# One table set for logarithms and exponentials, loaded by name, in an attention and SwiGLU kernel

## The chip, the cores and the metric

The kernel runs on one core of a Trainium2 chip. The metric is device time in microseconds of that core for one execution; the time before is the median of three runs. The engines are named as in the profile: PE (TensorE: matrix products), DVE (VectorE), ACT (ScalarE: activation functions, copies and some DMA issues), POOL (GpSimd) and SP (SyncE: issues most DMAs).

## The reference

Queries and keys are normalised row by row, attention runs over 8 batches with 12 heads, 448 positions and 64 columns, and its result goes through a SwiGLU block:

```python
def rmsnorm(x, g):
    rms = np.sqrt(np.mean(x * x, axis=-1, keepdims=True) + 1e-06)
    return x / rms * g
q_n, k_n = (rmsnorm(q, g_q), rmsnorm(k, g_k))
scores = scale * np.matmul(q_n, k_n.transpose(0, 1, 3, 2))
attn = np.exp(scores - np.max(scores, axis=-1, keepdims=True))
attn = attn / (np.sum(attn, axis=-1, keepdims=True) + 1e-09)
x = np.matmul(attn, v)          # then (B,H,S,D) -> (B*S, H*D) = (3584, 768)
g = x @ w_gate                  # w_gate, w_val: (768, 1536); w_out: (1536, 768)
silu = g * (1.0 / (1.0 + np.exp(-g)))
return silu * (x @ w_val) @ w_out
```

## The kernel before, in words

Two heads of one batch are a pair; there are 48 pairs. `attention(m)` adds the work of pair `m`: load queries and keys, square them on ACT, sum the squares on DVE, exchange partial sums between the partitions by four small copies on ACT (`ss`, L766), take one over the root (`inverse_root`), scale on POOL (L783), transpose on DVE, scale the queries on ACT (L802). Then come the scores on PE (L828, into the PSUM tile `st`, of which there are two), the exponentials on ACT (`exps`, L843, into `es`, `gt` or `more`), the weighted values on PE (L904, into `at`), the sums of the weights on PE (L928), their reciprocals on DVE (`rd`, L963), a copy (L983), an addition and a division.

`inverse_root` computes the root as exp(-0.5 ln(x)): a logarithm (L666) and an exponential (L667) of 28 columns on ACT, and an improvement on DVE (L672 to L674). ACT evaluates a function from the table set that is in use; where an activation needs a function of another set, the program has an `ACT_TABLE_LOAD` ahead of it, which the profile shows with the line of that activation. Silu (L1351) has a set of its own.

`block(n)` adds the SwiGLU block of two batches: up products (L1277) from weights in `ws` and inputs in `xs`, read out of PSUM by copies on ACT (L1238) and additions on DVE (L1240, L1242, L1244), then silu, then down products (L1456). Both matrix products are done by a scheme with 15 products for 9 blocks, whose combined weights are made by `convert` from raw 64-bit weights (loads L1104, ACT L1112 and L1116, DVE, POOL), stored to DRAM and loaded again as pieces of `ws` (L1372 for up, L1442 for down; two buffers).

The order on each engine is set by a planner, `Order`. Every step is added with its engine, an assumed duration, a due time (`when`), a `rank` that moves it ahead, what it follows, and the buffers that it takes and uses. `run` picks the steps one after the other; the program then has each engine's instructions in that order. A step may carry a `mode`; where it differs from its engine's mode, `SWITCH` is added to the step's end (1.3 on ACT). Before, the logarithms and roots carry the mode `"logarithms"` and silu the mode `"silu"`; the exponentials of the scores carry none. The first twelve pairs run alone; the other 36 run in three groups of twelve, each beside the down products of the block before it; between them stand the up products of the four blocks.

Of the kernel before, what the change touches and what calls it, by code (L numbers as in the profile page):

```python
# [9 lines left out]
F32 = mybir.dt.float32  # L10
U32 = mybir.dt.uint32
I64 = mybir.dt.int64
AF = mybir.ActivationFunctionType
# [347 lines left out]
class Order:  # L361
# [9 lines left out]

    SWITCH = dict(PE=0.17, ACT=1.3)

    def __init__(self, pools):
        self.pools = {name: [None] * n for name, n in pools.items()}
        self.turn = dict.fromkeys(pools, 0)
        self.users = {}
        self.pieces = []
        self.free = {}
        self.port = 0.0  # L380
        self.dma = 0.0
        self.last = {}
        self.mode = {}
# [37 lines left out]
    def run(self, lookahead=400):  # L421
        left = {}
        for piece in sorted(self.pieces, key=self.key):
            left.setdefault(piece["engine"], []).append(piece)
        while any(left.values()):
            best = None
            for engine, pieces in left.items():
                choice = None
                last = self.last.get(engine, dict(group=None))
                for piece in pieces[:lookahead]:  # L430
                    at = self.start(piece)
                    if at is None:
                        continue
                    if (
                        last["group"]
                        and piece["group"] == last["group"]
                        and at < self.free[engine] + 0.7
                    ):
                        choice = (at, piece)
                        break  # L440
                    if choice is None or at < choice[0] - 0.4:
                        choice = (at, piece)

                late = 0.7 if engine == "POOL" else 0.0
                if choice and (
                    best is None
                    or choice[0] + late < best[0] - 0.3
                    or choice[0] + late < best[0] + 0.3
                    and self.key(choice[1]) < self.key(best[1])
                ):  # L450
                    best = (choice[0] + late, choice[1])
            piece = best[1]
            at = self.start(piece)
            left[piece["engine"]].remove(piece)
            for key in piece["takes"]:
                ring = self.pools[key[0]]
                ring[self.turn[key[0]] % len(ring)] = key
                self.turn[key[0]] += 1
            end = at + piece["us"]
            if piece["mode"] and self.mode.get(piece["engine"]) != piece["mode"]:  # L460
                end += self.SWITCH[piece["engine"]]
                self.mode[piece["engine"]] = piece["mode"]
            self.last[piece["engine"]] = piece
            self.free[piece["engine"]] = end
            if piece["port"]:
                self.port = end
            if piece["kb"]:
                self.dma = max(self.dma, end) + piece["kb"] / 300.0
                end = self.dma + 1.8
            piece["at"], piece["end"] = at, end  # L470
            piece["emit"]()
# [3 lines left out]
def fast(  # L475
# [41 lines left out]
    nc = tc.nc  # L517
# [3 lines left out]
    P = 128  # L521
# [15 lines left out]
    const = ctx.enter_context(tc.tile_pool(name="const", bufs=1))  # L537
# [6 lines left out]
        qk=4, v=2, t=2, QT=2, KT=2, e=4, ea=7, eh=2, sums=1, inv=1, rd=1, rows=3, st=2, at=2, ss=2,  # L544
        rr=4, ws=2, **{x + str(i): 1 for x in "vw" for i in range(6)},
    )
    order = Order(BUFS)
    tiles = {}

    WORK, size = {}, 0  # L550
# [65 lines left out]
    gq2 = const.tile([P, 1], F32, name="gq2")  # L616
    gk2 = const.tile([P, 1], F32, name="gk2")
    gg = const.tile([P, 1], F32, name="gg")
    warm = const.tile([P, 1], F32, name="warm")

    LEAD, PAIR = 14.0, 10.0
    FIRST = LEAD + EARLY * PAIR + 6.0
    PRODUCT = 1.512
    UP, DOWN, BOTH = 30 * NG * PRODUCT, 90.7, 170.0

    MORE = 20.0
# [61 lines left out]
    def attention(m):  # L691
# [11 lines left out]
        early = m < EARLY  # L703
# [97 lines left out]
        def queries():  # L801
# [11 lines left out]
            uses=[("t", m), ("qk", (m, 0))],  # L813
        )
        qt = add(
            "ACT", 0.53, ready - 5.0, queries, after=[qt, gains], uses=[("qk", (m, 0))],
            takes=[("QT", m)],
        )

# [17 lines left out]
        def weights_of(j):  # L837
            return ("ea" if early else "e", (m, j)) if j < NJ - 1 else ("eh", m)
# [20 lines left out]
        for j in (3, 0, 1, 2):  # L859
            before = clusters.get((m - 2, "weighted" if j in (3, 0) else "total"))  # L860
            when = (ready + 0.3 if j in (3, 0) else base) + 0.01 * (j % 3)
            half = j == NJ - 1
            st = add(
                "PE", 0.41 if half else 0.76, when, lambda j=j: scores(j),
                after=[kt, qt, staged.get(ES), before],
                uses=[("KT", m), ("QT", m)], takes=[("st", (m, j))],
                group=("c", m - 1 if j in (3, 0) else m), mode="quarters",
            )
            ex[j] = add(
                "ACT", 0.5 if half else 0.92, when + 1.0, lambda j=j: exps(j),  # L870
                after=[st], uses=[("st", (m, j))],
                takes=[weights_of(j)],
            )
            if j in (1, 2) and not early:

                def more_sums(j=j):
                    if j == 1:
                        take("sums", m, [P, 2, S])
                    add_up(j)

                adds.append(
                    add(
                        "POOL", 2.15, when + 2.0, more_sums, after=[ex[j], ex[0], *adds[-1:]],
                        port=True, uses=[("e", (m, j)), ("e", (m, 0)) if j == 1 else ("sums", m)],
                        takes=[("sums", m)] if j == 1 else [],
                    )
                )
# [112 lines left out]
        if early:  # L1000
            inv = add(
                "PE", 0.82, when + SPREAD, spread_by_product, after=[inv], uses=[("rd", m)],
                mode="full",
            )
        else:
            inv = add(
                "ACT", 2.7, when + 4.5, spread, after=[inv, staged.get(SPARE)], uses=[("rd", m)],
                takes=[("inv", m)],
            )
        done_x[b, c] = add(  # L1010
            "DVE", 0.64, when + 5.0, divide, after=[inv, joined],
            uses=[] if early else [("inv", m)], port=not early,
        )
        if early:
# [15 lines left out]
    def sides(n, c, when):  # L1030

        x = {i: xs[:, slot, c] for i, slot in SLOT.items()}
        (a1, a2, a3), (b1, b2, b3) = ([x[i] for i in raw] for raw in RAW)
        for a in range(2):
            for k in range(3):
                side_done.setdefault((n, RAW[a][k]), []).append(done_x[2 * n + a, 3 * c + k])
        last = [done_x[2 * n + a, 3 * c + k] for a in range(2) for k in range(3)]
        for i, one, two, op in (
            (6, a1, a2, None),
            (8, a3, b2, ALU.subtract),  # L1040
            (1, b2, x[6], ALU.subtract),
            (10, x[1], b1, None),
            (13, a2, b2, ALU.add),
            (2, b3, b1, ALU.subtract),
            (3, x[2], a3, ALU.add),
            (12, x[3], a1, ALU.subtract),
            (9, a2, a3, ALU.add),
            (11, a3, b3, ALU.add),
            (4, b2, b3, None),
        ):  # L1050

            free = down_products.get((n - 1, 11), []) if i in (11, 12) else []
            last = [
                order.add(
                    "DVE", 0.64, when,
                    lambda to=x[i], one=one, two=two, op=op: combined(to, one, two, op),
                    after=[*last, *free], port=True,
                    rank=70.0 * (n == 0),
                )
            ]  # L1060
            side_done.setdefault((n, i), []).extend(last)
# [26 lines left out]

    def convert(key, src, order_of, to, when, place, by_bank):

        rank = 30.0 if by_bank else 0.0

        def add(*what, **more):
            return order.add(*what, **dict(rank=rank, **more))
# [6 lines left out]
        def load():  # L1101
# [6 lines left out]
        )  # L1108
        bits = dst.bitcast(U32)
        one = add(  # L1110
            "ACT", 1.2, when,
            lambda: nc.scalar.activation(dst, hi.bitcast(F32), AF.Copy, scale=2.0**-111),  # L1112
            after=[loaded],
        )
        two = add(
            "ACT", 1.2, when, lambda: nc.scalar.activation(lo, lo, AF.Copy, scale=2.0**-29),  # L1116
            after=[loaded],
        )

# [20 lines left out]
        last = one  # L1140
        for k in range(2):
            last = add(
                "DVE", 2.0 if by_bank else 1.85, when, lambda k=k: round_part(k), after=[last, two],
                takes=[bank] if by_bank and k == 0 else [], uses=[bank] if by_bank and k else [],
                port=not by_bank,
            )
# [399 lines left out]
    nc.gpsimd.memset(halves, 0.0)  # L1546
    for x in range(2):
        nc.gpsimd.memset(halves[ds(D * x, D), x], SCALE)
    nc.scalar.activation(warm, many[:, 0:1], AF.Ln)
    for t, x in ((gq2, g_q), (gk2, g_k)):  # L1550
        col = x.rearrange("(d one) -> d one", one=1)
        nc.scalar.dma_start(t[0:64, :], col)
# [96 lines left out]
```

## Time and profile before

| What | us |
|---|---|
| median of three runs | 1592.73 (1592.48 to 1594.61) |
| the profiled execution | 1595.54 |
| its span, first to last instruction | 1593.7 |
| ACT busy | 784.7 |
| of it table loads, 107 of 1.283 us | 137.3 |

A row of groups gives the line, engine and operation, what it writes and reads, the count, the busy time in us and the mean in ns, then the idle time just before and what ended it. A row of waits gives the engine and line that waited, what ended the wait, the sum in us, how many, and the longest. A row of the timeline gives start and length in us; in brackets stands the idle time of the engine before it. A row of windows gives the stretch, then the busy time of PE, PE's weight loads, DVE, ACT and POOL with counts, the granted TensorE clock, the DMA share and GB/s.

### The profile page before, as it was taken

The page shows a single profiled execution, that of the slowest core. Times are in us where ns is not written, and L with a number is a line of the kernel's source. Part 1 is how long each engine was busy: PE and PEld are TensorE (multiplying, and loading weights), DVE is VectorE, ACT ScalarE, POOL GpSimd, SP SyncE. Part 2 cuts the span into 40 slices and gives each one's busy share as a digit, 9 for nine tenths or more (in the row PEclk, how much of TensorE's full clock was granted, in tenths as well). Part 3 has the DMA queues.
Part 4 walks back from the last instruction along what each step waited for, and adds up shares of the span by engine and source line. Part 5 has one row for each costly group of instructions (what it writes and reads, how often), then busy time and mean ns, then how long its engine had stood idle before and what let it go on. Part 6 is the DMA issues. An engine that isn't in the chain of part 4 may idle for free. (4 is left out here: it accounts for less than half of the span.)

```text
span 1593.7 us, 19444 instructions
## 1 busy us (share of the span) xinstructions
PE 1464.4 (92%) x6672; PEld 686.0 (43%) x6672; DVE 903.3 (57%) x1405; ACT 784.7 (49%) x1452; POOL 404.3 (25%) x440
## 2 busy tenths in 40 slices
PE   3878889999888989999989989999999989999998
PEld 1333444444333445554434435554443335555554
DVE  2676877667675744444776654335676564333543
ACT  5886443336877532127678632226788732222100
POOL 1343467444443310002344410001353320000000
PEclk9788999999999999999999999999999999999999
DMA  6467698894343332234344242244353342222235
GB/s 136 113 145 195 216 321 268 268 250 124 84 111 70 80 98 99 99 96 126 84 95 99 64 118 79 91 121 104 83 113 73 94 120 79 85 81 99 79 91 100
DMA packets 408241, 193.29 MB, mean 121 GB/s; under 512 B 324164, under 2 KB 397892, under 8 KB 398404
## 3 DMA queue, kind: packets, MB, share of 16 engines
q1 hardware_dynamic: 288288, 163.92, 36.9%
q10 hardware_dynamic: 119844, 28.04, 8.2%
q8 instruction: 54, 0.88, 0.2%
q14 instruction: 55, 0.45, 0.1%
HBM read 157.29 MB, written 34.60 MB: 120 GB/s over the span
## 5 line engine op out<-in xcount | busy, mean ns | idle before, releaser
L1277 PE MATMUL mm<-xs,ws 128*128 128x448 f32 x960 | 408.8, 548 | 21.8 <-DVE xs L1024 8.9
L1277 PE MATMUL at<-xs,ws 128*128 128x448 f32 x960 | 408.5, 549 | 3.8 <-DVE v L1244 3.2
L1277 PEld LDWEIGHTS mm<-xs,ws 128*128 128x128 f32 x960 | 183.9, 193 | 208.6 <-issue 170.0
L1277 PEld LDWEIGHTS at<-xs,ws 128*128 128x128 f32 x960 | 185.2, 193 | 188.7 <-issue 177.5
L783 POOL TENSOR_TENSOR work<-work,rr 128x448 f32<-128x448 f32 x96 | 101.5, 1076 | 649.9 <-DMA v<-in_v_dram 322.0
L828 PE MATMUL st<-work 64*64 64x448 f32 (+1 forms) x1536 | 165.4, 533 | 67.4 <-ACT es L843 31.6
L1456 PE MATMUL mm<-gt,ws 128*128 128x448 f32 x448 | 176.1, 544 | 0.8 <-DVE spare L1244 0.8
L1240 DVE TENSOR_TENSOR gt<-gt,mm 128x448 f32<-128x448 f32 x64 | 39.6, 618 | 204.8 <-PE mm L1277 204.8
L1456 PE MATMUL mm<-hs,ws 128*128 128x448 f32 x384 | 154.3, 553 | 0.0
L1351 ACT ACTIVATE st<-gt 128x448 f32<-128x448 f32 x96 | 52.4, 547 | 196.2 <-DVE gt L1244 94.7
L843 ACT ACTIVATE es<-st 128x896 f32<-128x896 f32 x129 | 114.3, 913 | 50.8 <-PE at L904 20.8
L978 ACT COPY spare<-rd 32x224 f32<-32x224 f32 x288 | 108.1, 375 | 53.8 <-DVE rd L963 48.1
L904 PE MATMUL at<-es,v 64*64 64x448 f32 x1032 | 114.7, 559 | 7.4 <-ACT es L843 4.3
L1456 PEld LDWEIGHTS mm<-gt,ws 128*128 128x128 f32 x448 | 83.5, 190 | 84.6 <-issue 81.8
L1238 ACT COPY gt<-mm 128x448 f32<-128x448 f32 x80 | 42.6, 533 | 156.2 <-PE mm L1277 152.9
L828 PEld LDWEIGHTS st<-work 64*64 64x64 f32 x1536 | 50.4, 138 | 155.9 <-ACT es L843 48.9
L848 POOL TENSOR_TENSOR sums<-es 128x896 f32<-128x896 f32 x36 | 76.0, 2111 | 124.8 <-PE st L928 82.3
L1456 PEld LDWEIGHTS mm<-hs,ws 128*128 128x128 f32 x384 | 72.4, 194 | 74.6 <-issue 72.2
L1238 ACT COPY v<-at 128x448 f32<-128x448 f32 x96 | 51.0, 531 | 76.5 <-PE at L1277 68.1
L848 POOL TENSOR_TENSOR sums<-sums,es 128x896 f32<-128x896 f32 x36 | 79.0, 2196 | 2.8
L799 DVE STREAM_TRANSPOSE work<-work 128x448 f32<-128x448 f32 x96 | 59.6, 628 | 32.0 <-POOL work L783 31.8
L904 PEld LDWEIGHTS at<-es,v 64*64 64x64 f32 x1032 | 40.6, 137 | 68.7 <-issue 54.6
(141 smaller groups left out, 1670.3 us busy)
## 6 DMA issues: line engine op xcount, KB each, us to landing
ws<-up_sides SPq DMA_DIRECT2D x48, 1280.0 KB, 5.7
ws<-down_sides SPq DMA_DIRECT2D x28, 1024.0 KB, 5.0
work<-in_q_dram SPq DMA_DIRECT2D x192, 56.0 KB, 2.4
work<-in_k_dram SPq DMA_DIRECT2D x180, 56.0 KB, 2.3
out_dram<-spare ACTq DMA_DIRECT2D x168, 56.0 KB, 2.0
v<-in_v_dram SPq DMA_DIRECT2D x96, 96.0 KB, 2.4
es<-in_moe_w_out_dram SPq DMA_DIRECT2D x9, 384.0 KB, 8.0
v<-in_v_dram SPq DMA_DIRECT2D x96, 32.0 KB, 2.3
```

Source lines behind the costliest of these rows:

```text
L783: nc.gpsimd.tensor_tensor(out=tiles["t", m][:, x], in0=tiles["qk", (m, x)], in1=rr.to_broadcast([P, NC, C]), op=ALU.mult,)
L799: nc.vector.transpose(to, tiles["t", m][:, x].rearrange("p c f -> p (c f)"))
L828: nc.tensor.matmul(st[ds(D * x, D), h, 0:n], tiles["KT", m][rows, ds(P * j + D * of_keys, D)], tiles["QT", m][rows, ds(Q * of_queries, n)] ...
L843: nc.scalar.activation(e, tiles["st", (m, j)][:, :, 0 : S * width(j) // P], AF.Exp)
L848: nc.gpsimd.tensor_tensor(out=to, in0=tiles["e", (m, 0)] if j == 1 else to, in1=e, op=ALU.add)
L904: nc.tensor.matmul(tiles["at", (m, x)][ds(D * h, D), queries], tiles["v", m][rows, j, h], tiles["e", (m, j)][rows, h], start=j == 0, stop= ...
L978: nc.scalar.copy(inv[ds(D * h + C * to, C), ts(x, Q)], tiles["rd", m][ds(D * h + C * x, C)])
L1238: nc.scalar.copy(to, ps)
L1240: nc.vector.tensor_tensor(out=to, in0=old, in1=ps, op=ALU.add)
L1277: nc.tensor.matmul(ps(), w[:, step % 5, which, c], xs[:, SLOT[x], c], start=fresh and c == 0, stop=c == NC2 - 1, skip_group_check=True,)
L1351: nc.scalar.activation(take(*act, [P, 2, TB])[:, 0, 0:S], to, AF.Silu)
L1456: nc.tensor.matmul(banks[s][:, 0:S], w[:, step % 2, s, g], where[x][:, g], start=fresh and g == 0, stop=g == NG - 1, skip_group_check=True,)
```

## The change

The planner calls a function when ACT enters the mode `"logarithms"`. That function loads the set `natural_log_exp_and_others` by name. ACT begins in that mode, the exponentials of the scores carry it too, and the activation `warm` at the start is replaced by the load. Besides, some assumed durations and one rank of the planner change.

```diff
-    def __init__(self, pools):
+    def __init__(self, pools, begin):
+        self.begin = begin
...
             if piece["mode"] and self.mode.get(piece["engine"]) != piece["mode"]:
                 end += self.SWITCH[piece["engine"]]
                 self.mode[piece["engine"]] = piece["mode"]
+                if piece["mode"] in self.begin:
+                    self.begin[piece["mode"]]()
...
-    order = Order(BUFS)
+    def load_tables():
+        nc.scalar.preload_act_table_set("natural_log_exp_and_others")
+
+    order = Order(BUFS, dict(logarithms=load_tables))
...
-    PRODUCT = 1.512
+    PRODUCT = 1.504
...
-            "ACT", 0.53, ready - 5.0, queries, after=[qt, gains], uses=[("qk", (m, 0))],
+            "ACT", 0.65, ready - 5.0, queries, after=[qt, gains], uses=[("qk", (m, 0))],
...
                 "ACT", 0.5 if half else 0.92, when + 1.0, lambda j=j: exps(j),
                 after=[st], uses=[("st", (m, j))],
-                takes=[weights_of(j)],
+                takes=[weights_of(j)], mode="logarithms",
...
-                "ACT", 2.7, when + 4.5, spread, after=[inv, staged.get(SPARE)], uses=[("rd", m)],
+                "ACT", 3.0, when + 4.5, spread, after=[inv, staged.get(SPARE)], uses=[("rd", m)],
...
     def convert(key, src, order_of, to, when, place, by_bank):
-        rank = 30.0 if by_bank else 0.0
+        rank = 20.0 if by_bank else 0.0
...
-            "ACT", 1.2, when,
+            "ACT", 1.28, when,
...
-                "DVE", 2.0 if by_bank else 1.85, when, lambda k=k: round_part(k), after=[last, two],
+                "DVE", 2.28 if by_bank else 1.85, when, lambda k=k: round_part(k), after=[last, two],
...
-    nc.scalar.activation(warm, many[:, 0:1], AF.Ln)
+    load_tables()
+    order.mode["ACT"] = "logarithms"
```

The division's and the combinations' assumed durations on DVE change in the same way (0.64 to 0.71, 0.66 or 0.86). In the changed kernel the lines of `attention` stand 6 further down: L666 becomes L672, L843 becomes L849, L1104 becomes L1110.

On ACT, in the first mixed stage near 490 us of the profile: `ss` are the partial sums of squares, `rr` the roots, `rd` the reciprocals, `es` and `more` the exponentials, `st` the scores. Before:

```order
L978 COPY spare<-rd 32x224 x8
L766 COPY ss<-ss 32x28 x4
L666 ACT_TABLE_LOAD
L666 ACTIVATE rr<-ss 128x28
L667 ACT_TABLE_LOAD
L667 ACTIVATE rr<-rr 128x28
L802 ACTIVATE work<-work,gg 128x448
L843 ACTIVATE es<-st 128x896 x2
L843 ACTIVATE more<-st 128x448
```

and now, for the same pair:

```order
L772 COPY ss<-ss 32x28 x4
L808 ACTIVATE work<-work,gg 128x448
L672 ACTIVATE rr<-ss 128x28
L673 ACTIVATE rr<-rr 128x28
L849 ACTIVATE es<-st 128x896 x2
L989 COPY xs<-at 128x448
L849 ACTIVATE more<-st 128x448
```

The two loads are gone, the scaling of the queries stands ahead of the logarithm, and a copy stands between the exponentials.

On ACT, towards the end of the first twelve pairs near 133 us of the profile, with the same names and `xs` for the attention's result. Before:

```order
L766 COPY ss<-ss 32x28 x4
L666 ACT_TABLE_LOAD
L666 ACTIVATE rr<-ss 128x28
L667 ACT_TABLE_LOAD
L667 ACTIVATE rr<-rr 128x28
L983 COPY xs<-at 128x448
L843 ACTIVATE more<-st 128x448
L843 ACTIVATE es<-st 128x896
```

and now:

```order
L772 COPY ss<-ss 32x28 x4
L989 COPY xs<-at 128x448
L672 ACTIVATE rr<-ss 128x28
L673 ACTIVATE rr<-rr 128x28
L748 ACTIVATE work<-work 128x448
L849 ACTIVATE more<-st 128x448
L849 ACTIVATE es<-st 128x896
```

The copy moved ahead of the logarithm, and one square (L748) stands ahead of the exponentials.

On SP, in the first up stage near 285 us of the profile, where it issues loads of raw weights (into `hs`, `es`, `spare`, `work`) and of the pieces of `ws`. Before:

```order
L1104 DMA spare<-in_moe_w_out_dram 128x3x128 x3
L1104 DMA hs<-in_moe_w_out_dram 128x3x128 x3
L1104 DMA es<-in_moe_w_out_dram 128x3x128 x3
L1372 DMA ws<-up_sides_85 128x2560
L1104 DMA work<-in_moe_w_out_dram 128x3x128 x3
```

and now:

```order
L1110 DMA spare<-in_moe_w_out_dram 128x3x128 x3
L1110 DMA hs<-in_moe_w_out_dram 128x3x128 x3
L1378 DMA ws<-up_sides_85 128x2560
L1110 DMA es<-in_moe_w_out_dram 128x3x128 x3
L1110 DMA work<-in_moe_w_out_dram 128x3x128 x3
```

The piece of `ws` moved ahead of the raw weights into `es`.

More of the change, by code (lines that the diff above doesn't have):

```diff
@@ L618, in fast @@
     gg = const.tile([P, 1], F32, name="gg")
-    warm = const.tile([P, 1], F32, name="warm")
     LEAD, PAIR = 14.0, 10.0
     FIRST = LEAD + EARLY * PAIR + 6.0
-    PRODUCT = 1.512
+    PRODUCT = 1.504
     UP, DOWN, BOTH = 30 * NG * PRODUCT, 90.7, 170.0
@@ L1010, in attention @@
         done_x[b, c] = add(
-            "DVE", 0.64, when + 5.0, divide, after=[inv, joined],
+            "DVE", 0.64 if early else 0.71, when + 5.0, divide, after=[inv, joined],
             uses=[] if early else [("inv", m)], port=not early,
@@ L1054, in sides @@
                 order.add(
-                    "DVE", 0.64, when,
+                    "DVE", 0.66 if op else 0.86, when,
                     lambda to=x[i], one=one, two=two, op=op: combined(to, one, two, op),
@@ L1115, in convert @@
         two = add(
-            "ACT", 1.2, when, lambda: nc.scalar.activation(lo, lo, AF.Copy, scale=2.0**-29),
+            "ACT", 1.28, when, lambda: nc.scalar.activation(lo, lo, AF.Copy, scale=2.0**-29),
             after=[loaded],
```

## The prediction

> **What bounds the kernel now.** I read the busy shares first, then the same shares cut by stage, then who waits for whom in each stage, and at last the timeline around single waits.
>
> ```profile
> PE 1464.4 (92%) x6672; PEld 686.0 (43%) x6672; DVE 903.3 (57%) x1405; ACT 784.7 (49%) x1452; POOL 404.3 (25%) x440
> ```
>
> PE is busy for 1464.4 of 1593.7 us, so all that can be won without less work on PE lies in the other 129 us and in the clock. ACT's 49% is a mean over unlike stages. By stage (us of busy time behind each engine, then the granted TensorE clock and the DMA share):
>
> ```profile
> 0.00:173.50 173.50, 121.00 (x1201) 51.12 (x1202) 99.39 (x175) 121.48 (x205) 57.97 (x93) 0.90 0.59 142
> 173.50:374.00 200.50, 186.26 (x469) 91.17 (x468) 151.67 (x229) 86.47 (x123) 114.98 (x206) 0.96 0.87 269
> 374.00:560.00 186.00, 163.99 (x1047) 67.78 (x1046) 124.47 (x186) 137.28 (x270) 72.07 (x45) 0.98 0.40 89
> 760.00:940.00 180.00, 169.47 (x1072) 75.35 (x1071) 120.32 (x178) 124.01 (x246) 66.35 (x38) 0.99 0.41 91
> 1140.00:1314.00 174.00, 161.10 (x1002) 70.60 (x994) 111.99 (x165) 121.18 (x246) 66.35 (x38) 0.98 0.42 94
> ```
>
> The first row is the attention of the first twelve pairs of heads alone: ACT is as busy as PE (121 us each), and PE idles for 52.5. Rows 3, 4 and 5 are attention mixed with down products: PE idles for 22.0, 10.5 and 12.9 us there, with ACT at 69 to 74%. Row 2 is the first up products, where PE idles for 14.2. What ACT spends on table loads:
>
> ```profile
> L667 ACT ACT_TABLE_LOAD x48 | 61.6, 1283 | 0.9
> L666 ACT ACT_TABLE_LOAD x47 | 60.3, 1283 | 3.9 <-DMA work<-in_k_dram 3.1
> L1351 ACT ACT_TABLE_LOAD x9 | 11.5, 1283 | 6.2 <-DVE st L1135 6.1
> L843 ACT ACT_TABLE_LOAD x2 | 2.6, 1283 | 4.1 <-PE at L904 4.1
> L1549 ACT ACT_TABLE_LOAD x1 | 1.3, 1283 | 1.6 <-PEq L1633 1.6
> ```
>
> These are 107 loads of 1.283 us, 137.3 us, 17% of ACT's busy time. 95 of them are one pair's logarithm (L666) and exponential (L667), each of which fetches its own set. Whether they hurt is seen in one place, in order of time:
>
> ```profile
> 1199.56 1.28 ACT L666 ACT_TABLE_LOAD   x1
> 1200.85 0.23 ACT L666 ACTIVATE rr<-ss 128x28 f32<-128x28 f32 x1
> 1201.09 1.28 ACT L667 ACT_TABLE_LOAD   x1
> 1202.39 0.23 ACT L667 ACTIVATE rr<-rr 128x28 f32<-128x28 f32 x1
> 1202.52 1.70 ACT L843 ACTIVATE es<-st 128x896 f32<-128x896 f32 x2
> 1203.47 2.58 PE L828 MATMUL st<-work 64*64 64x224 f32 x16 [3.92 <-ACT es L843]
> ```
>
> Two loads (2.57 us) stand right ahead of the exponentials of the scores (L843), whose end frees the PSUM tile `st` that PE's next scores need: PE stood idle for 3.92 us. The waits of PE on ACT (sum, times, longest), first in stage 1:
>
> ```profile
> PE st L828 <- ACT work L802: 22.5, 4, 19.5
> PE st L828 <- ACT more L843: 6.2, 2, 4.1
> PE at L904 <- ACT es L843: 4.3, 2, 2.7
> PE st L828 <- ACT es L843: 2.1, 2, 1.8
> ```
>
> in the first mixed stage:
>
> ```profile
> PE st L828 <- ACT es L843: 9.8, 7, 3.8
> PE st L828 <- ACT more L843: 4.6, 3, 2.2
> PE st L928 <- ACT more L843: 2.9, 3, 1.1
> ```
>
> and the largest row of the second, then of the third:
>
> ```profile
> PE st L828 <- ACT es L843: 9.1, 9, 3.3
> ```
>
> ```profile
> PE st L828 <- ACT es L843: 9.2, 8, 3.9
> ```
>
> **The change, part by part.** The list of the changed program has 22 loads: one at the start, eleven ahead of silu, ten back from it. So 85 go, 85 x 1.283 = 109 us of ACT. What counts is only the part that PE waits for.
>
> Mixed stages. In the first of them the three rows give 9.8 + 4.6 + 2.9 = 17.3 us. I went through these waits on ACT's timeline: nearly all have two loads just ahead. From the two longest only 2.57 us can go. One is the 3.8 above, the other this:
>
> ```profile
> 462.79 1.02 PE L828 MATMUL st<-work 64*64 64x224 f32 x8 [3.07 <-ACT es L843]
> ```
>
> 17.3 - 1.3 - 0.5 = 15.5. In the second, 9.1 less 0.7 (3.3 - 2.57), less some 0.9 of short waits of 0.2 that are only the exponential's own length, and less this one, behind four output DMAs that ACT issues:
>
> ```profile
> 897.14 0.61 PE L828 MATMUL st<-work 64*64 64x224 f32 x8 [0.96 <-ACT es L843]
> ```
>
> leaves 6.5. The third has the same pattern, with 3.9 as its longest: 9.2 - 1.3 - 1.4 = 6.5. Together 28.5 us.
>
> Stage 1. 6.2 + 4.3 + 2.1 us, of which 1.5 (4.1 - 2.57), 0.1 (2.7 - 2.57) and a short 0.3 stay: 10.7. One more wait there, 1.67 us on a copy behind two loads, is in the rows further down: 12.4. The first pair's load ahead of its exponential lies on the way to the first matmul, which PE awaits for the 19.5 us above:
>
> ```profile
> 13.79 1.28 ACT L667 ACT_TABLE_LOAD   x1
> ```
>
> 1.3 us more. The load that the removed `warm` activation had, and the load by name in its place, stand ahead of this idle time and cost nothing:
>
> ```profile
> 10.22 1.04 ACT L742 ACTIVATE work<-work 128x448 f32<-128x448 f32 x2 [7.15 <-DMA v<-in_v_dram]
> ```
>
>
> The clock. Sixteen matmuls of L828 took 2.58 us after that 3.92 us gap; undisturbed they take this:
>
> ```profile
> 1213.14 1.67 PE st L828 x16
> ```
>
> So 0.9 us comes back for each of the mixed stages' three gaps of 3.3 to 3.9 us, 2.7 in all. In stage 1 the granted clock is 0.90, some 12 of 121 us. A stretch of it, and the waits in it:
>
> ```profile
> 65.00:75.00 10.00, 8.32 (x52) 2.94 (x56) 8.23 (x12) 8.31 (x14) 5.93 (x8) 0.66 0.36 66
> ```
>
> ```profile
> 65.35 0.97 PE L904 MATMUL at<-es,v 64*64 64x448 f32 x4 [1.67 <-ACT xs L983]
> 67.64 1.01 PE L904 MATMUL at<-es,v 64*64 64x448 f32 x2 [1.32 <-DVE xs L986]
> ```
>
> The clock fell to 0.66 although the gaps are 1.67 and 1.32 us. Between 0 and 12 us I take 5, since about as much of PE's idle time there goes as stays. [...]
>
> [...]
>
> Sum: 28.5 + 12.4 + 1.3 + 2.7 + 5 = 50 us. Against it stands what is late next: ACT still issues output DMAs and eight small copies per pair ahead of exponentials, as in the 0.96 us wait above. Nothing to 25 us of the sum could go that way; I take 5, since few waits are of that kind today. Net 45.
>
> The planner's other numbers (product 1.504, queries 0.65, spreading 3.0, conversions 1.28 and rank 20, exponentials in the mode of the logarithms) cost nothing by themselves; they only reorder. The sequences shown with the change tell how little: on ACT a pair's order is the same but for a copy or the queries' scaling. On SP one load of `ws` now stands ahead of three loads of raw weights instead of behind them:
>
> ```profile
> 285.59 4.85 SPq L1104 DMA_DIRECT2D es<-in_moe_w_out_dram  x3
> ```
>
> so it is issued up to 4.85 us sooner, and those three DMAs later by one issue and by its wait for a free buffer; they feed down weights, which are first used in the mixed stage from 374 us on. A lower rank of the conversions on DVE touches what PE waits for in the first up stage, whose largest row is
>
> ```profile
> PE mm L1277 <- DVE gt L1244: 8.3, 3, 3.7
> ```
>
> All of it may go, or as much may come: -8.3 to +8.3, taken as 0. The two added silu switches per run (nine loads to eleven) fall where products fill PE; at worst 2 x 2.57 = 5 us.
>
> The profiled execution took 1595.54 us, 1.8 outside its span, and the median of the runs is 1592.73, 2.8 below it. 1595.5 - 45 - 2.8 = 1547.7: I predict **1548 us**.
>
> **The rivals.** First, half is handed on: with the loads gone, PE waits for the DMA issues and copies on ACT, or for DVE's improvement of the roots, and only 25 us remain: 1568. For it: 57% of DVE and in-order queues; against it: the waits sit on ACT's exponentials, with loads straight ahead.
>
> Second, more comes: a plan whose ACT costs agree with the chip also orders PE better, and what stays of the waits goes too, with all the clock: the 9 us of waits left out above (1.8, 2.6 and 2.7 in the mixed stages, 1.9 in stage 1), the other 7 of stage 1's clock, the 8.3 on DVE, and nothing of the 5 is handed on, 29 us in all: 1519.
>
> Third, the clock does not come back: without the 5 and the 2.7 us, 1556. [...]
>
> Fourth, slower: the stream of converted weights becomes the bound of the first up stage. It starts about 19 us earlier, with a DMA share of 0.87 already. A piece of `ws` feeds ten products (the chain has one of them here), 15.0 us, and lands 5.7 us after its issue; the last row is SP's longest hold ahead of such an issue:
>
> ```profile
> 1321.89 1.50 PE mm L1277 x4
> ```
>
> ```profile
> ws<-up_sides SPq DMA_DIRECT2D x48, 1280.0 KB, 5.7
> ```
>
> ```profile
> SPq L1372 <- DMA up_sides<-hs: 13.4, 2, 12.7
> ```
>
> That leaves 9.3 us for SP to be held up, and one hold of 12.7 passed without a wait of PE on a DMA. The gain is lost once nine pieces (the three later groups of weights) each come 5 us later than PE can bear; at 6 us, 1602. Against it: conversions start when attention ends, so they move with it.
>
> Fifth, no change: every wait removed comes back as another, 1592. That the loads stay in the program is excluded by its list.
>
> **How the numbers follow.** The forecast (1538 to 1555) has 0.42, half 0.20, more 0.20, no clock 0.10, no change 0.04, slower 0.04. Less than 0.2% (3.2 us) cannot be told from nothing here. Faster by more: 0.92; same 0.04; slower 0.04. The range holds the forecast and its three faster or weaker neighbours with the unknown 8.3 us around them: 1517 to 1574.
>
> **What would show it.** The groups of loads at the logarithm's and the exponential's lines are gone, and 22 loads of 1.283 us remain; ACT's busy time falls by 109 us to about 676, or the first step is wrong. The first product of the up stage starts near 155 instead of 173.5, with a clock above 0.93 in the stage ahead of it, or stage 1 is wrong. The three mixed stages last about 170, 173 and 167 us, with PE's waits on L843 at a third of today's, or the step on the mixed stages is wrong. A new row of waits of L1277 on a DMA, or of L828 on DVE or POOL, would be the rival that takes it.

## The result, and the profile after

The changed kernel takes 1532.1 us (median of 4 runs, 1531.2 to 1535.5) against 1593.7 in the same job: a ratio of 0.962, 95% interval 0.960 to 0.9635, 61.6 us less. The forecast was 1548, its own band 1538 to 1555 and the range 1517 to 1574: the time lies in the range, 6 us below the band. Of the changed kernel's page, the busy times:

```profile
PE 1439.6 (94%) x6672; PEld 683.1 (45%) x6672; DVE 912.1 (60%) x1405; ACT 679.7 (44%) x1366; POOL 397.0 (26%) x440
```

ACT is busy 105 us less, but PE as well: 24.8 us less for the same 6672 matmuls. Most of that is the clock, as the first experiment shows (19.6 of 22.0 us there), the part of the gain that the forecast had too small. The loads that are left:

```profile
L552 ACT ACT_TABLE_LOAD x11 | 14.1, 1283 | 2.9 <-PEq L1640 1.6 <-issue 1.2
L1357 ACT ACT_TABLE_LOAD x11 | 14.1, 1283 | 0.2
```

The first three stages, cut where the first up product and the first down product begin, of the kernel before (its first stage was shown) and then of the changed one:

```profile
173.50:381.50 208.00, 192.87 (x497) 93.59 (x495) 158.43 (x241) 90.65 (x130) 114.98 (x206) 0.96 0.85 262
381.50:576.20 194.70, 172.38 (x1093) 72.09 (x1089) 126.59 (x185) 137.07 (x275) 75.75 (x46) 0.98 0.41 92
```

```profile
0.00:152.00 152.00, 110.42 (x1201) 49.39 (x1202) 99.59 (x175) 92.35 (x181) 57.50 (x92) 0.97 0.68 164
152.00:367.50 215.50, 190.66 (x490) 92.09 (x489) 158.16 (x239) 87.87 (x127) 115.02 (x207) 0.95 0.82 253
367.50:539.00 171.50, 167.80 (x1097) 72.19 (x1096) 133.17 (x190) 115.01 (x262) 75.65 (x46) 1.00 0.47 103
```

The first stage is 21.5 us shorter, the first mixed stage 23.2, and the first up stage 7.5 longer. PE's waits on ACT are nearly gone; in the first mixed stage of the changed kernel these are all its waits on the exponentials:

```profile
PE st L834 <- ACT es L849: 1.9, 6, 0.6
PE st L834 <- ACT more L849: 1.2, 1, 1.2
PE st L934 <- ACT es L849: 0.4, 1, 0.4
```

3.5 us where 17.3 and a few smaller ones stood. What became longer is PE's wait on DVE in the first up stage, the changed kernel's largest row there (8.3 us before):

```profile
PE mm L1283 <- DVE gt L1250: 17.2, 4, 9.6
```

### The profile page after: what moved, and what is told of

The parts are those of the page before. It is cut to its first block, busy times and chain, and to the rows that moved or that the text cites. A ratio compares the mean times of both kernels' runs of the same rounds, so it can differ in the third digit from the quotient of the medians.

```text
span 1529.4 us, 19374 instructions
## 1 busy us (share of the span) xinstructions
PE 1439.6 (94%) x6672; PEld 683.1 (45%) x6672; DVE 912.1 (60%) x1405; ACT 679.7 (44%) x1366; POOL 397.0 (26%) x440
## 4 chain that ended last, share of the span: by engine, by line
PE 65%; DVE 5%; ACT 2%; issue 2%; DMA 1%; ACTq 1%; SPq 1%; POOL 0%; DVEq 0%; POOLq 0%
PE mm L1283 18%; PE at L1283 18%; PE mm L1462 18%; PE st L834 5%; PE at L910 4%; ACTq L1520 1%; PE st L934 1%; ACT spare L984 1%; ACT es L849 1%; DMA out_dram<-spare 1%; DVE spare L1510 1%; DVE sums L860 1%; DVE rd L969 1%; DMA ws<-down_sides 0%; DVE xs L996 0%
## 5 line engine op out<-in xcount | busy, mean ns | idle before, releaser
L1283 PEld LDWEIGHTS mm<-xs,ws 128*128 128x128 f32 x960 | 182.8, 192 | 218.4 <-issue 167.2
L834 PE MATMUL st<-work 64*64 64x448 f32 (+1 forms) x1536 | 154.6, 508 | 29.3 <-ACT work L808 20.4
L1462 PE MATMUL mm<-hs,ws 128*128 128x448 f32 x384 | 151.0, 544 | 0.0
L849 ACT ACTIVATE es<-st 128x896 f32<-128x896 f32 x129 | 114.4, 914 | 80.0 <-PE at L910 31.0
L1357 ACT ACTIVATE st<-gt 128x448 f32<-128x448 f32 x96 | 52.5, 547 | 205.1 <-DVE gt L1250 96.2
L834 PEld LDWEIGHTS st<-work 64*64 64x64 f32 x1536 | 51.7, 134 | 104.8 <-issue 36.3
L854 POOL TENSOR_TENSOR sums<-sums,es 128x896 f32<-128x896 f32 x36 | 75.7, 2103 | 2.8
L1360 DVE SCALAR_TENSOR_TENSOR gt<-st,v 128x448 f32<-128x448 f32 x96 | 59.7, 622 | 16.9 <-ACT st L1357 10.0
```

The lines of the kernel that those rows point to most:

```text
L834: nc.tensor.matmul(st[ds(D * x, D), h, 0:n], tiles["KT", m][rows, ds(P * j + D * of_keys, D)], tiles["QT", m][rows, ds(Q * of_queries, n)] ...
L849: nc.scalar.activation(e, tiles["st", (m, j)][:, :, 0 : S * width(j) // P], AF.Exp)
L854: nc.gpsimd.tensor_tensor(out=to, in0=tiles["e", (m, 0)] if j == 1 else to, in1=e, op=ALU.add)
L1283: nc.tensor.matmul(ps(), w[:, step % 5, which, c], xs[:, SLOT[x], c], start=fresh and c == 0, stop=c == NC2 - 1, skip_group_check=True,)
L1357: nc.scalar.activation(take(*act, [P, 2, TB])[:, 0, 0:S], to, AF.Silu)
L1360: nc.vector.scalar_tensor_tensor(to, tiles[act][:, 0, 0:S], 1.0 / SCALE, tiles[ready], op0=ALU.mult, op1=ALU.mult,)
```

## The experiments

The change has two parts: no loads between logarithm and exponential, and a new order from the planner's new numbers. The first four runs take them apart.

**Only the loads.** Every engine's order as before; each place where a logarithm, an exponential or a silu is issued says which set it needs, and a load by name is issued only where the set differs.

```diff
+    def need(name):
+        if name == "logarithms" and table[0] != name:
+            nc.scalar.preload_act_table_set("natural_log_exp_and_others")
+        table[0] = name
...
+            need("logarithms")
             nc.scalar.activation(rr, ss, AF.Ln, scale=GAIN**-2)
```

> The order of every engine as before, and only the table loads as in the change: 18 loads instead of 107 (the set for logarithms and exponentials is named at the start and after silu). Theory 1, the loads themselves held PE up and held its clock down: at least four fifths of the 61.6 us are there without any new order, 1530 to 1545 us, with the granted clock of the first 150 us near 0.97. Theory 2, the reordering that follows from the planner's new numbers carries a good part: 1560 us or more. The first up stage tells something of its own: if it is lengthened by starting earlier, its waits on DVE are here too (205.7 us before, 215.6 after); if the new order does it, the stage stays at 206.

1531.3 us, ratio 0.961 (0.959 to 0.963): the whole gain, with no new order at all. (The expectation's 205.7 and 215.6 are by slightly other cuts; by the cuts above the first up stage lasted 208.0 us before and 215.5 in the changed kernel.) The first stages and the sum of its windows:

```profile
0.00:146.30 146.30, 107.80 (x1201) 47.36 (x1202) 99.52 (x175) 92.66 (x181) 58.84 (x93) 0.99 0.70 168
146.30:352.50 206.20, 192.01 (x497) 93.44 (x495) 158.46 (x241) 89.30 (x130) 115.13 (x206) 0.96 0.85 265
352.50:532.20 179.70, 169.76 (x1093) 72.25 (x1089) 128.14 (x185) 111.39 (x253) 75.97 (x46) 0.99 0.45 99
```

```profile
sum 1529.60, PE 1442.40; mean PE 160.27
```

This kernel differs from the one before by nothing but loads (and the activation `warm` that one of them replaces), so it splits the gain of its profiled span, 1593.7 - 1529.6 = 64.1 us: PE's idle time falls from 129.3 to 87.2, 42.1 us of waits, and its busy time from 1464.4 to 1442.4, 22.0 us.

How much of the 22.0 us is clock can be read from the clock records of the traces, which begin near 30 us and hold two values in these runs, 1.00 and 0.50: four products took 1.67 us at 1.00 (the changed kernel at 300.70 us) and 3.35 at 0.50 (at 315.35 us, shown further below). PE did 75.7 us of its work at half clock before and 36.5 without the loads. These four products took twice as long at half clock; by an estimate with this factor, the clock explains (75.7 - 36.5) / 2 = 19.6 us. The other 2.4 stay unexplained.

The first up stage is 206.2 us long although it starts 27 us earlier, so the earlier start is not what lengthens it.

**Only the new order.** The changed kernel, with each function fetching its own set.

```diff
-    order = Order(BUFS, dict(logarithms=load_tables))
+    order = Order(BUFS, {})
...
-    load_tables()
+    nc.scalar.activation(warm, many[:, 0:1], AF.Ln)
```

> The order of the changed kernel, with each function fetching its own set again (111 loads instead of 22). Theory 1: back to about the time of before, 1583 to 1605 us. Theory 2: the new order keeps a good part of the gain, 1565 us or less.

1589.6 us, ratio 0.998 (0.9965 to 0.9996). As a whole, the order is worth 0.2% with the loads; without them the two kernels agree (ratios 0.961 and 0.962, in two jobs).

**The conversions' numbers undone** in the changed kernel.

```diff
-        rank = 20.0 if by_bank else 0.0
+        rank = 30.0 if by_bank else 0.0
...
-                "DVE", 2.28 if by_bank else 1.85, ...
+                "DVE", 2.0 if by_bank else 1.85, ...
```

> The changed kernel with the planner's numbers of the conversions as before (rank 30, 1.2 and 2.0). If these numbers put the conversions where DVE's reads of products wait behind them in the first up stage (17.2 us of waits of PE on one line against 8.3), the stage falls back to about 206 us and the time to 1520 to 1526. If the earlier start of the stage does it, the time stays within 3 us of 1532.

1533.9 us, and the first up stage lasts 219.9 us. These numbers alone are not what lengthens it. Which of the others does was not tried one by one; with the old numbers for the first twelve pairs and the conversions, in the mixture further below, the stage lasts 202.9 us. The timeline of the changed kernel shows what happens there, at PE's longest wait:

```profile
301.83 5.20 ACTq L1199 DMA_DIRECT2D down_sides<-spare  x3
...
307.07 0.55 ACT L1357 ACTIVATE st<-gt 128x448 f32<-128x448 f32 x1 [7.40 <-DMA down_sides<-spare]
307.65 0.62 DVE L1360 SCALAR_TENSOR_TENSOR gt<-st,v 128x448 f32<-128x448 f32 x1 [2.64 <-ACT st L1357]
...
309.99 0.75 DVE L1138 TENSOR_SCALAR st<-work 128x576 uint32<-128x576 uint32 x1
...
314.00 0.75 DVE L1144 CUSTOM_DVE_ANT_0 work<-work,st 128x1152 uint16<-128x1152 uint16 x1
314.68 0.62 DVE L1250 TENSOR_TENSOR gt<-mm,gt 128x448 f32<-128x448 f32 x1
...
315.35 3.35 PE L1283 MATMUL mm<-xs,ws 128*128 128x448 f32 x4 [9.60 <-DVE gt L1250]
```

A silu on ACT stands behind three DMA issues; DVE waits for it with everything queued behind; then DVE runs six steps of a conversion (310.0 to 314.7) before the read that frees PE's bank. PE waits for 9.6 us, in the end on DVE's read, not on a piece of `ws`. Why ACT's three issues took 5.20 us, where the next three took 1.61 (at 309.91 us), these rows do not show.

**Loads in the first stage only.** The changed kernel, with loads by name put back for twelve pairs.

```diff
+            if m < EARLY:
+                load_tables()
             nc.scalar.activation(rr, ss, AF.Ln, scale=GAIN**-2)
+            if m < EARLY:
+                load_tables()
             nc.scalar.activation(rr, rr, AF.Exp, scale=-0.5)
```

> The changed kernel, with two loads by name put back ahead of the logarithm and the exponential of the first twelve pairs alone (24 loads more, 30.8 us of ACT). Theory 1: the first stage is back at 170 to 174 us and the rest as in the changed kernel, 1548 to 1555 us. [...]

1550.8 us. The stage is back at 172.6 us, and all later stages are as in the changed kernel to 1 us:

```profile
0.00:172.60 172.60, 117.48 (x1200) 51.06 (x1201) 99.69 (x175) 122.66 (x205) 57.74 (x93) 0.92 0.60 144
```

Idle time 55.1 against 41.6 us, busy time 117.5 against 110.4, clock 0.92 against 0.97: of 20.6 us between these two executions, 13.5 are waits and 7.1 busy time. The stage lost clock again; the lowest was 0.51 from 90 to 100 us, where PE's longest gaps were 3.06 and 1.85 us. Two drops behind shorter gaps are shown below, at half the dose.

**Loads in the later stages only** (the same edit with `m >= EARLY`).

> The changed kernel with two loads by name put back ahead of the logarithm and the exponential of the later 36 pairs alone. Theory 1, stages add up: the first stage and the first up stage stay as in the changed kernel, and the rest loses what the kernel with all loads lost beyond the kernel with loads in the first stage only: 1532 + (1589.6 - 1550.8) = 1571, 1565 to 1577 us. Rival, the stages lean on each other (a late pair makes the next stage late): 1580 or more, or under 1560.

1571.8 us (1563.3 to 1572.7), where 1571 was the sum. The first stage (PE's busy time, the clock, the DMA share and GB/s):

```profile
0.00:156.00 156.00, 115.30 (x1201) 0.94 0.67 160
```

It took 156.0 us instead of the changed kernel's 152.0, though its idle time is no longer (40.7 against 41.6 us): its clock was 0.94 instead of 0.97. The stages behind it lost 36.3 us, where 38.9 were to be lost. So the stages add up to some 4 us, and that the sum fits within 1 us is partly luck.

**Half the dose.** The kernel with only the loads removed, and one load by name back ahead of each pair's exponential.

```diff
+            nc.scalar.preload_act_table_set("natural_log_exp_and_others")
             nc.scalar.activation(rr, rr, AF.Exp, scale=-0.5)
```

> The old order without its loads, and one load by name put back ahead of each pair's exponential: half the dose. Each gap of PE that had two loads ahead shrinks by 1.28 us; what is left of the idle time, worked out from the gaps of before, is about 14 of the 42 us. If the clock falls only after single long gaps, none of which is left but those with other causes, it stays as without loads: about 1545 us, with a busy PE of some 108 us in the first stage. If the sum of short gaps brings it down, it gives back a third of its 22 us too: about 1552 us, with some 112 us in the first stage. If time is linear in the number of loads: 1561 us.

1562.0 us, half of the way back: the linear estimate of 1561 held, and that of 1552 missed. The profiled span of 1556.2 us has 105.9 us idle, 18.7 more than without the loads where 14 were worked out from the gaps, and PE is busy for 1450.3 us, 7.9 more. Only about half of that is clock: PE did 44.6 us of its work at half clock against 36.5, which costs 4.1 us. That is neither the nothing of the first theory nor the 7.3 (a third of 22) of the second. Two 10 us stretches of this kernel (PE's busy time, the clock, the DMA share and GB/s), and PE's rows where the second begins:

```profile
90.00:100.00 10.00, 7.89 (x99) 1.00 0.60 115
100.00:110.00 10.00, 9.52 (x96) 0.83 0.87 214
```

```profile
99.81 1.78 PE L976 MATMUL mm<-rd,chosen 128*128 128x224 f32 x4 [2.11 <-DVE rd L971]
101.52 3.36 PE L912 MATMUL at<-es,v 64*64 64x448 f32 x24
```

From 88 to 110 us no gap is longer than 2.11 us, and yet the clock drops to 0.83, and 24 matmuls of the weighted values take 3.36 us. Cut finer, the drop is 3.41 us at half clock:

```profile
96.51:99.92 3.41, 1.30 (x17) 1.00 0.64 154
99.92:103.33 3.41, 3.41 (x16) 0.50 1.02 279
103.33:106.75 3.42, 3.42 (x56) 1.00 0.90 244
```

The 0.66 in the prediction's stretch of the kernel before is 6.83 us at half clock, and in the 3.41 us ahead of it the clock was 1.00:

```profile
63.31:66.72 3.41, 1.34 (x12) 1.00 0.73 201
66.72:73.55 6.83, 5.91 (x32) 0.50 0.34 56
```

In both cases PE was idle for some 2.1 of the 3.41 us ahead of the drop: in one gap here, in a gap of 1.67 us and part of the next one there. So it took no long gap for the clock to fall here, and the sum of the short gaps did not give its cost either. Which short gaps cost clock and which do not was not shown.

**A better mixture.** The old numbers for the first twelve pairs, conversions and products, the new ones for the rest, without loads.

```diff
+            "ACT", 0.53 if early else 0.65, ready - 5.0, queries, ...
+                takes=[weights_of(j)], mode=None if early else "logarithms",
+                    "DVE", 0.64 if n == 0 else 0.66 if op else 0.86, when, ...
```

> No loads but at switches; the old planner's numbers for the first twelve pairs and the conversions, so that every engine's order up to the first down products is the old one, and the new numbers for the later 36 pairs (queries 0.65, spreading 3.0, division 0.71, combinations 0.66 and 0.86, exponentials in the mode of the logarithms). If the two halves of the order are worth what they seem (first up stage 206 instead of 215.5 us by the old, first mixed stage 171.5 instead of 179.7 and second up stage 191.4 instead of 198 by the new), the sum is 1531 - 15 = 1516 us, 1512 to 1522. If the better later stages were only the other side of a later first up stage, it stays at 1528 to 1534.

> As the kernel with old early and new late numbers, but with only the mode of the exponentials, the spreading and the combinations new, and the queries and the division old. If these three carry the gain of the later stages: within 3 us of that kernel. If not: 1525 us or more.

1523.5 and 1525.1 us, ratios 0.9575 (0.954 to 0.961) and 0.9586 (0.955 to 0.962). The first mixed stage takes 171.3 us as hoped and the first up stage 202.9, but the second up stage stays at 197.3, so the halves add up only in part. Whether the three numbers carry it is not decided: 1525.1 is within 3 us of the other kernel, as they should give, but also at the 1525 that was to speak against them. To set it against the changed kernel, both ran again in one job:

> The changed kernel again, beside the kernel with old early and new late numbers and on the same chip: 1530 to 1534 us, ratio to before 0.960 to 0.964.

> The kernel with old early and new late numbers again. If its gain over the changed kernel is real: 1518 to 1526 us and at least 0.3% under the changed kernel in the same job. If it was one chip's scatter: within 0.2% of it.

1532.4 us, ratio 0.9623 (0.9606 to 0.9639), against 1522.1 us, ratio 0.9566 (0.955 to 0.958): the mixture is faster than the kernel before and, by 0.6%, than the changed one. The first stage of the changed kernel in this execution:

```profile
0.00:157.70 157.70, 115.38 (x1201) 50.78 (x1202) 99.72 (x175) 92.76 (x182) 58.03 (x93) 0.94 0.66 160
```

The same instructions took 152.0 us in the execution shown first, with 110.4 us of busy time and a clock of 0.97; the idle time is nearly the same (42.3 and 41.6 us). So the clock of one stage can differ by 5 us between two executions, and a difference of that size between single stages, as the 7.1 us above, is not settled by one profile of each. The effect of the loads is larger: in the first stage PE did 21.3 to 31.0 us of its work at half clock in the three kernels with two loads per pair there, and 0.6 to 14.4 us in the eight executions without them.

## Why the prediction was right, point by point

| Term of the sum, us | forecast | only loads removed |
|---|---|---|
| waits in stage 1, with the first pair's load | 13.7 | 14.0 |
| waits in the first mixed stage | 15.5 | 12.4 |
| waits in the second and third | 13.0 | 14.1 |
| clock in stage 1 | 5 | 13.2 |
| clock elsewhere | 2.7 | 8.8 |
| handed on to what is late next | -5 | none seen |

The right column is PE's idle and busy time by stage of the kernel before against the kernel with only its loads removed. In the two rows of the clock it is the change of the busy time; by the clock records 13.5 and 6.1 us of it are clock.

*The waits.* Right in what was counted: taking each wait of PE that had two loads ahead, and no more than the loads' 2.57 us of it, gave 42.2 us, and 42.1 are measured, 40.5 of them in the stages named and the rest in the up stages. That the sums agree to 0.1 us is luck. The first mixed stage gave 3.1 us less than forecast and the other stages more. One of its two longest waits was misread: the 3.07 us at 462.79. On ACT, four output DMAs stand ahead of the exponentials that end it, and no loads; the pair's loads come behind them.

```profile
456.88 3.29 ACTq L1514 DMA_DIRECT2D out_dram<-spare  x4
...
461.82 0.92 ACT L843 ACTIVATE es<-st 128x896 f32<-128x896 f32 x1
462.76 1.28 ACT L666 ACT_TABLE_LOAD   x1
```

Without the loads this wait is still there:

```profile
425.36 0.76 PE L834 MATMUL st<-work 64*64 64x224 f32 x8 [2.77 <-ACT es L850]
```

Of the 2.57 us that were counted on it 0.3 came, and that is most of the 3.1 us.

*The clock.* That waits which go give clock back was right, and the size was not: 7.7 us against 22.0 of busy time, 19.6 of it clock. The step that failed is "about as much of PE's idle time there goes as stays", which made the lost clock a share of the idle time. In stage 1 only 14.0 of 52.5 us of idle time went, and yet nearly all of the loss: the work at half clock fell from 31.0 to 3.9 us and the clock rose from 0.90 to 0.99. So the lost clock was no fixed share of the idle time here. The mixed stages' term counted 0.9 us behind each of three long gaps; PE's busy time fell in each of these stages, by 2.3 to 3.6 us.

*The clock that does not come back* is out: 19.6 us of it came back. Short gaps did cost clock: with one load per pair it was 0.50 from 99.92 to 103.33 us, with no gap over 2.11 us since 88 us.

*The loss of 5 us* did not come in the sum. What ACT issues ahead of exponentials still costs PE single waits: the 2.77 us above, and 2.0 us at most in the later mixed stages of the changed kernel.

*The price of a load* was right: 1.283 us, with less than 0.02 us on either side where ACT had work waiting (17 to 19 ns ahead and 11 to 12 ns behind in the kernel before).

*The planner's numbers at nothing.* Right for the sum and wrong in its parts. Against the kernel with only the loads removed, the new order costs 5.7 us in stage 1 (11.4 by the second execution) and 9.3 in the first up stage, and wins 8.2 in the first mixed and 6.6 in the second up stage. The bound of 8.3 us for DVE's reads was a little short: PE's idle time in the first up stage went from 15.1 to 24.8, by the same cuts. That the sum is nothing is luck, as the mixture shows.

*The slower rival* was wrong in its mechanism. The first up stage did become longer, but no wait of PE there is on a transfer, and it is as long (218.4 us) with all loads back and a start at 171.6.

*More than forecast*, the second rival at 1519, named two of the right terms: more clock, and nothing handed on in the sum. The better order was not among the causes, and neither the 9 us of further waits nor the 8.3 on DVE came.

## What to carry to other kernels

Where one pair of functions alternates on ACT, look in the list of instructions for table loads between them and name a set that has both; price them not by ACT's busy share but by the waits of the bounding engine that have a load just ahead, each no further than the loads' length. Look at each such wait on that engine's timeline, since one counted here had DMA issues ahead and stayed. When waits of PE go, count PE's busy time too: here 19.6 of the 64.1 us were clock. And change a planner's numbers apart from such a fix, since a new order can win in one stage what it loses in another.

## What the runs showed of the hardware that was not expected

With one load per pair the TensorE clock fell to 0.50 for 3.41 us (99.92 to 103.33 us), where no gap of PE since 88 us had been longer than 2.11 us. With the loads alone removed, the granted clock in stage 1 went from 0.90 to 0.99 when 14.0 of 52.5 us of idle time went. A load of the set that was already in use took as long as any other here: with the 24 put back by name in the first stage, the mean of this line's 35 loads is still 1283 ns.

```profile
L552 ACT ACT_TABLE_LOAD x35 | 44.9, 1283 | 5.1 <-DMA work<-in_k_dram 1.7 <-PEq L1644 1.6 <-issue 1.2
```
